# A linear-attention and two-layer feed-forward kernel: mish by tanh, arctan and sine in grouped table loads, 30 matmul tiles from float32 to fp32r, weights parked as two halves

## Chip, cores and metric

One Trainium2 chip, one of its cores. The time is device microseconds of one launch, from several runs of the same program; a profile is one further execution taken by the hardware profiler. Engines are called as the profile calls them: PE (matmul), PEld (its weight loads), DVE, ACT, POOL, SP (which issues the DMAs here).

## The reference

Inputs are float32 or wider: r, k, v of shape (4 batches, 8 heads, 768 steps, 48), decays w and bonuses u per head, and two feed-forward layers whose weights come in float64 (the kernel reads them as pairs of 32-bit words).

```python
# attention, per batch b and head h, state is 48x48
for t in range(768):
    cur = outer(u * k[t], v[t])
    y[t] = r[t] @ (state + cur)
    state = w[:, None] * state + outer(k[t], v[t])
x = y as (4 * 768 tokens, 384)
h = x @ w_in                       # 384 -> 2048
x = (h * tanh(log1p(exp(h)))) @ w_out     # mish, 2048 -> 384
h = maximum(x @ w2_in, 0)          # 384 -> 2048
out = (h * h) @ w2_out             # 2048 -> 384
```

## The kernel before

**Tiles and blocks.** The 768 steps are cut into six chunks c of 128; a chunk of all four batches is 512 tokens. The attention of a chunk is computed by units (chunk, batch), 24 in all. The feed-forward layers work on one chunk at a time: a *block* is (layer, chunk), and `BLOCKS` (L171) is their order: (1,0), (1,1), (2,0), (2,1), (1,2), (1,3), (2,2), ... and so on, so that two chunks pass through layer 1, then the same two through layer 2. A block has 16 *tiles* j of 128 hidden features (`NF` = 16). For tile i (numbered through all 192 of the kernel) `up` (L839) multiplies the tile's 128x384 weights by the 384x512 input into one PSUM buffer h; `act1` (L863) or `act2` (L905) does the activation on ACT and DVE; `down1` (L913) or `down2` (L949) multiplies its output by the tile's second weights and adds to three or four accumulators over the 16 tiles.

**Precision.** A float32 matmul of 512 columns shows as two records. The other way, `mm3` (L832), splits both operands into a high part, rounded to fp32r, and a low part (the rest): three fp32r matmuls, high by high, high by low, low by high. The split is `halves` (L892) for activations, ACT making the high copy (L896, L898) and DVE subtracting (L901); `split_w` (L375) for weights; `split_x` (L805) for a block's input. Two constants say what stays float32: `FULL_UP = (0,)` and `FULL_DOWN = (0, 1)` (L239). Block 0 is float32 in its ups (L848) and downs (L926); block 1 is fp32r in its ups and in the downs of tiles 0 to 7 and float32 in the downs of tiles 8 to 15. That is 16 up and 24 down tiles in float32, all others in fp32r.

**Mish.** Per 128x512 tile in `act1`:

```python
ACT e = exp(h / ws)                  # L880
ACT e = square(e + 1)                # L881, the 1 is a one-column tile
DVE e = min(e, SQ20) + 1             # L871
ACT r = ln(e)                        # L883
ACT r = exp(-r)                      # L884
DVE e = e * r                        # L885
DVE r = (e - 2) * r                  # L874
DVE g = (r + 0.5) * h                # L877, and half a factor later in finish1
```

Exp, ln, square and copy are all in one activation table, loaded once at the start (L279).

**Weights.** `convert` (L323) turns a tile's 768 weight columns from float64 words to float32: ACT scales the high word (L337) and extracts bits (L344, layer 1), DVE shifts and merges (L348 to L358). The raw tile comes by one DMA of 768 KB (L331). For layer 1 the float32 tile lands in the ring `wa` (pairs of tiles), where block 0 uses it directly; during block 0 it is also written to DRAM (`keep`, L383) and split for block 1. Raw tiles go through a ring `wb` of eight. Layer 2's weights are converted and split while block 1 and the first layer-2 block run (`make_w2`, L388), and both halves are parked in DRAM. When the order comes back to layer 1, `again_w1` (L396) loads the float32 tile and splits it again on ACT and DVE; `again_w2` (L404) loads the two halves in two DMAs.

**Attention.** A unit scales r and k (L439), forms scores on PE (L494), fills a diagonal tile (L469 on ACT, four records per fill; for chunk 0 every second on POOL), selects by mask (L505, DVE), multiplies (L543 to L605) and updates the state. `SPANS` (L173) says beside which feed-forward tiles a chunk's units are due: chunk 1 beside tiles 0 to 13. Chunk 0 comes first, with nothing beside it; its outputs x are copied from PSUM to a float32 tile (L644 on ACT, L646 on DVE).

**Order.** Every step is an item of a `Plan` (L80) with engine, estimated duration, due time and the tiles it reads and writes. `order` (L108) plays the engines through in time: when an engine is free it takes, of the items whose inputs are ready, the one with the smallest due time. The resulting list is the program order of each engine, SP's DMAs included. Tiles live in rings; an item that reuses a buffer waits for all users of the tile before it. Rings that matter here: `e` 3, `ghi` 3, `glo` 3, `wf` 2, PSUM `up` 2 and `flex` 1 for h, `at` 2 for attention. An up of tile i is due at i, its activation at i+1, its down at i+4 (`LAG`).

## Time and profile before

| what | value |
|---|---|
| three runs | 935.93, 936.21 (median), 936.94 us |
| profiled execution, span from first to last instruction | 935.9 us |
| first up matmul of block 0, of block 1, of block 2 | 34.61, 126.82, 199.68 us |
| last matmul starts | 928.88 us |
| busy: PE, PEld, DVE, ACT, POOL | 910.3, 734.7, 597.2, 619.4, 8.5 us |
| DMA | 114.00 MB, mean 122 GB/s |

A profile is read engine by engine and by stage. Busy time of PE is the union of matmul records whose ends are modelled, so the pace of a dense stretch is read from start to start. DVE and ACT records overlap a little with the next one. Stages here are cut at the first up matmuls of blocks 0, 1 and 2.

### The profile page before, as it was taken

To read this page: it belongs to the slowest core of one execution; us is meant where nothing else is said; L and a number is where in the kernel's file an instruction comes from. 1 tells how busy PE (TensorE), PEld (TensorE's weight loads), DVE (VectorE), ACT (ScalarE), POOL (GpSimd) and SP (SyncE) were. 2 spreads that over 40 slices of the span, in tenths; PEclk is the share of its full clock that TensorE was granted. 3 is DMA by queue.
4 is the path that set the end of the run, shared out by engine and by line. 5 is a ranking of instruction groups with operands and counts; after the bars stand their busy time and mean duration, and the time that the engine had idled before them with its cause. 6 is when DMAs were issued, how large, how long until landed. Compare 5 with 4: busy or idle time off the path is not lost.

```text
span 935.9 us, 13341 instructions
## 1 busy us (share of the span) xinstructions
PE 910.3 (97%) x5072; PEld 734.7 (78%) x5072; DVE 597.2 (64%) x981; ACT 619.4 (66%) x1126; POOL 8.5 (1%) x18
## 2 busy tenths in 40 slices
PE   3999999999999999999999999999999999999997
PEld 3645458768988888878888889888878888899996
DVE  6899999999544648688876332354777877211212
ACT  1897779777646767778777554667777877544442
POOL 2100000000000000000000000000000000000000
PEclk9999999999999999999999999999999999999999
DMA  9994153788423434010666220434100155200001
GB/s 247 348 333 139 44 173 132 244 268 311 171 79 113 139 113 130 1 54 1 216 212 213 80 71 1 131 100 130 51 9 1 68 202 178 92 1 1 34 1 39
DMA packets 40875, 114.00 MB, mean 122 GB/s; under 512 B 4609, under 2 KB 7938, under 8 KB 40802
## 3 DMA queue, kind: packets, MB, share of 16 engines
q1 hardware_dynamic: 40802, 113.06, 36.7%
q8 instruction: 42, 0.69, 0.3%
q14 instruction: 31, 0.25, 0.1%
HBM read 88.47 MB, written 23.59 MB: 120 GB/s over the span
## 4 chain that ended last, share of the span: by engine, by line
PE 92%; DVE 3%; ACT 1%; DMA 1%; issue 1%; SPq 0%; DVEq 0%
PE h L833 13%; PE h L835 13%; PE h L834 13%; PE acc L960 8%; PE acc L962 7%; PE acc L961 7%; PE acc L926 6%; PE acc L833 5%; PE acc L835 5%; PE acc L834 5%; PE h L848 3%; PE sc L494 2%; PE y L566 2%; DMA rk<-in_rk_dram 1%; PE y L543 1%
## 5 line engine op out<-in xcount | busy, mean ns | idle before, releaser
L901 DVE TENSOR_TENSOR glo<-g,ghi 128x512 fp32r<-128x512 f32 x96 | 66.3, 691 | 211.8 <-ACT ghi L896 211.5
L909 ACT ACTIVATE e<-h 128x512 f32<-128x512 f32 x96 | 57.3, 597 | 115.4 <-PE h L835 114.9
L896 ACT ACTIVATE ghi<-e 128x512 fp32r<-128x512 f32 x96 | 60.5, 630 | 57.0 <-PE acc L961 55.7
L833 PE MATMUL h<-xh_a,w 128*128 128x512 f32 x216 | 87.7, 406 | 2.1 <-DVE e L877 2.1
L880 ACT ACTIVATE e<-h 128x512 f32<-128x512 f32 x96 | 57.2, 597 | 47.8 <-PE h L835 42.3
L833 PE MATMUL acc<-ghi,w 128*128 128x512 f32 x216 | 86.1, 398 | 0.0
L835 PE MATMUL h<-xh_a,w 128*128 128x512 f32 x216 | 85.0, 394 | 0.0
L835 PE MATMUL acc<-ghi,w 128*128 128x512 f32 x216 | 84.7, 392 | 0.0
L834 PE MATMUL h<-xl_a,w 128*128 128x512 f32 x216 | 84.2, 390 | 0.0
L834 PE MATMUL acc<-glo,w 128*128 128x512 f32 x216 | 84.1, 389 | 0.0
L885 DVE TENSOR_TENSOR e<-e,r 128x512 f32<-128x512 f32 x96 | 65.9, 688 | 23.2 <-ACT r L884 22.8
L883 ACT ACTIVATE r<-e 128x512 f32<-128x512 f32 x96 | 60.2, 631 | 21.7 <-DVE e L871 21.6
L881 ACT ACTIVATE e<-e,one 128x512 f32<-128x512 f32 x96 | 69.5, 725 | 2.0
L469 ACT ACTIVATE A<-cst_sb,dg 128x128 f32<-128x128 f32 x176 | 55.9, 402 | 18.3 <-DVE dg L454 18.3
L874 DVE SCALAR_TENSOR_TENSOR r<-e,r 128x512 f32<-128x512 f32 x96 | 65.8, 687 | 1.6
L926 PE MATMUL acc<-g,wf 128*128 128x512 f32 x144 | 65.9, 595 | 0.0
L910 ACT ACTIVATE g<-e 128x512 f32<-128x512 f32 x96 | 60.7, 632 | 2.9
L901 DVE TENSOR_TENSOR glo<-e,ghi 128x512 fp32r<-128x512 f32 x72 | 49.4, 689 | 20.3 <-ACT ghi L898 18.7
L884 ACT ACTIVATE r<-r 128x512 f32<-128x512 f32 x96 | 60.2, 629 | 1.4
L898 ACT ACTIVATE ghi<-e 128x512 fp32r<-128x512 f32 x72 | 45.0, 626 | 12.5 <-DVE e L877 12.2
L833 PEld LDWEIGHTS h<-xh_a,w 128*128 128x128 f32 x216 | 40.5, 188 | 12.8 <-DVE e L877 3.6
L877 DVE SCALAR_TENSOR_TENSOR e<-r,h 128x512 f32<-128x512 f32 x72 | 49.1, 684 | 1.4
(291 smaller groups left out, 2102.4 us busy)
## 6 DMA issues: line engine op xcount, KB each, us to landing
raw<-in_w_dram SPq DMA_DIRECT2D x32, 768.0 KB, 5.9
nat<-in_nat_dram SPq DMA_DIRECT2D x24, 576.0 KB, 5.9
wk<-wd SPq DMA_DIRECT2D x32, 384.0 KB, 3.1
rk<-in_rk_dram SPq DMA_DIRECT2D x24, 448.0 KB, 5.5
wd<-wf SPq DMA_DIRECT2D x16, 384.0 KB, 7.4
wd2hi<-w SPq DMA_DIRECT2D x16, 384.0 KB, 5.0
wd2lo<-w SPq DMA_DIRECT2D x16, 384.0 KB, 3.8
out_dram<-o SPq DMA_DIRECT2D x24, 192.0 KB, 1.9
```

What stands on the lines that cost most here:

```text
L833: nc.tensor.matmul(o, wh, xh, start=first, stop=False, skip_group_check=True)
L834: nc.tensor.matmul(o, wh, xl, start=False, stop=False, skip_group_check=True)
L835: nc.tensor.matmul(o, wl, xh, start=False, stop=last, skip_group_check=True)
L874: nc.vector.scalar_tensor_tensor(r.ap, e.ap, 2.0, r.ap, ALU.subtract, ALU.mult)
L881: add("ACT", 0.73, d + 0.2, lambda: nc.scalar.activation(e.ap, e.ap, AF.Square, bias=one), r=[e, T_one], w=[e])
L885: add("DVE", 0.69, d + 1, lambda: nc.vector.tensor_tensor(e.ap, e.ap, r.ap, ALU.mult), r=[e, r], w=[e])
L901: lambda: nc.vector.tensor_tensor(lo.get(), g.ap, f32v(hi.ap), ALU.subtract), r=[g, hi], w=[lo],
L910: add("ACT", 0.63, d + 0.2, lambda: nc.scalar.activation(g.get(), e.ap, AF.Square), r=[e], w=[g])
L926: nc.tensor.matmul(o, ws_[0][:, sl], hi.ap, start=(j == 0), stop=(j == NF - 1), skip_group_check=True)
L960: nc.tensor.matmul(o, hi[:, sl], h_, start=(j == 0), stop=False, skip_group_check=True)
L961: nc.tensor.matmul(o, hi[:, sl], l_, start=False, stop=False, skip_group_check=True)
L962: nc.tensor.matmul(o, lo[:, sl], h_, start=False, stop=(j == NF - 1), skip_group_check=True)
```

## The change

In blocks 0 and 1 (tiles 0 to 31) mish is computed from t = (1 - tanh(x/2))/2, which is 1/(1 + e^x): tanh(log1p(e^x)) = (1 - t²)/(1 + t²) = cos(2 arctan t) = sin(pi/2 - 2 arctan t). Tanh, arctan and sine are not all in one table: three tables hold (tanh, arctan), (arctan, sine) and (sine, tanh). Tiles go in groups of 1, 1, six times 2 and six times 3; a group's tanhs, arctans and sines run as batches, and a pass over the finished program order puts a table load before a pass whose function the loaded table lacks, taking the table that lasts longest. Tanh then arctan then sine, repeated, takes three loads for two groups. Mish costs DVE one multiply per tile. From tile 32 on the mish is as before, with a bias of 1.0 given as an immediate.

Only the downs of tiles 0 to 9 stay float32 (`FULL`). For that block 0's input is split, and its weights. All layer-1 weights are split once, in `convert`, and both halves are parked in DRAM and loaded again as one tile of 768 KB; so are layer 2's. Each weight tile j has one buffer `w{j}` that holds first the raw words, then the two halves; the float32 form is in a ring `wf` of 6. Rings `e`, `ghi` and `glo` have 4. In block 1 h goes around five PSUM buffers (`up` 2, `flex` 1, `at` 2). The high copies of activations of tiles 0 to 31, of layer-1 weights 2 to 15, and every second diagonal fill of chunk 1 move from ACT to DVE. Options that were off are removed from the code.

```diff
+HALFPI = 1.5707963267948966
+GROUPS = (1, 1) + (2,) * 6 + (3,) * 6
+TRIG = sum(GROUPS)
+GROUP_OF = [(sum(GROUPS[:g]), n) for g, n in enumerate(GROUPS) for _ in range(n)]
+HIGH, WHIGH = 32, 2
+FULL = frozenset(range(0, 10))
...
+TABLES = (
+    ("sigmoid_and_others", "TA"), ("trig_and_small", "AS"), ("silu_and_others", "ST"),
+    ("natural_log_exp_and_others", "EL"),
+)
+def table_loads(items):
+    users = [it for it in items if it["table"]]
+    loads, k = {}, 0
+    while k < len(users):
...
+        best = max(TABLES, key=run)
+        loads[users[k]["n"]] = best[0]
+        k = run(best)
+    return loads
...
-        (w_p, "wa", NF // 2), (w_p, "wb", NF // 2),
-        (conv_p, "raw", 2), (conv_p, "wf", 2),
+        *((w_p, f"w{j}", 1) for j in range(NF)),
+        (conv_p, "wf", 6),
...
-        (f_p, "e", 3), (f_p, "r", 2), (f_p, "ghi", 3), (f_p, "glo", 3), (f_p, "o", 4),
+        (f_p, "e", 4), (f_p, "r", 2), (f_p, "ghi", 4), (f_p, "glo", 4), (f_p, "o", 4),
...
+        if layer == 1 and j >= WHIGH:
+            add("DVE", 0.56, due, lambda: nc.vector.tensor_copy(hi.get(), f.get()), r=[f], w=[hi])
+        else:
+            add("ACT", 0.87, due, lambda: nc.scalar.activation(hi.get(), f.get(), AF.Copy), r=[f], w=[hi])
         add(
-            "DVE", 0.15 + n, due + 0.5,
-            lambda: nc.vector.tensor_tensor(lo.get(), f.get()[:, cols], f32v(hi.get()), ALU.subtract), r=[f, hi], w=[lo],
+            "DVE", 0.96, due + 0.5,
+            lambda: nc.vector.tensor_tensor(lo.get(), f.get(), f32v(hi.get()), ALU.subtract), r=[f, hi], w=[lo],
         )
-    def keep(x, j, t, due):
-        d = kept[x, j] = fixed(wd[x][j], f"wd{x}_{j}")
-        it = add("SP", 0.393, due, lambda: dma(d.ap, t.get() if x == "1" else f32v(t.get())), r=[t], w=[d])
+    def keep(layer, j, due):
+        d = kept[layer, j] = fixed(wd[layer][j], f"wd{layer}_{j}")
+        t = W[layer, j][0].whole
+        it = add("SP", 0.786, due, lambda: dma(d.ap, f32v(t.get())), r=W[layer, j], w=[d])
...
+    def again(layer, j, due):
+        d = kept[layer, j]
+        t, hi, lo = parts(layer, j, "r")
+        add("SP", 0.786, due, lambda: dma(f32v(t.get()), d.ap), r=[d], w=[hi, lo])
...
+        if units[n][0] == 1 and not e:
+            def g():
...
+                nc.vector.tensor_tensor(
+                    A.get(), anti[:, None, :].to_broadcast([128, NP, C]), d[:, :, None].to_broadcast([128, NP, C]), ALU.mult
+                )
+            add("DVE", 0.69, due, g, r=[u["dg"], T_cst], w=[A])
+            return
...
+            def g():
+                a, o = (direct["all", x].get()[:, :, cols] for x in ("xh", "xl"))
+                i = y[0][:, 0:3 * C].rearrange("q (k t) -> q k t", t=C)
+                nc.vector.tensor_tensor(o, i, f32v(a), ALU.subtract)
+            add("DVE", 0.55, due, g, r=[y[0]] + direct["xh"], w=direct["xl"])
...
+    def turn(i, extra=0.0):
+        b = GROUP_OF[i][0] if i < TRIG else i
+        return b + 0.02 * (i - b) + extra
...
-        h = R["flex" if flex else "up"].new([128, 512], F32, f"h{i}")
+        name = ("up", "up", "flex", "at", "at")[i % 5] if NF <= i < TRIG else "flex" if flex else "up"
+        h = R[name].new([128, 512], F32, f"h{i}")
...
+        if i < TRIG:
+            add(
+                "ACT", 0.6, turn(i, 1),
+                lambda: nc.scalar.activation(e.get(), h.ap, AF.Tanh, scale=0.5 / ws), r=[h], w=[e], table="T",
+            )
...
+                def a():
+                    for _, x, _, _ in now:
+                        nc.scalar.activation(x.ap, x.ap, AF.Arctan, scale=-0.5, bias=0.5)
...
+                for k, (n, x, o, p) in enumerate(now):
+                    add(
+                        "ACT", 0.64 + (k == 0), -50 + i + 0.1 * k,
+                        lambda x=x: nc.scalar.activation(x.ap, x.ap, AF.Sin, scale=-2.0, bias=HALFPI), r=[x], w=[x],
+                        table="S",
+                    )
+                for n, x, o, p in now:
+                    add(
+                        "DVE", 0.69, turn(n, 2),
+                        lambda x=x, o=o, p=p: nc.vector.tensor_tensor(o.get(), x.ap, p.ap, ALU.mult), r=[x, p], w=[o],
+                    )
+                    late.append((n, o, None) if n in FULL else (n, *halves(n, o, turn(n, 2.2))))
...
+            if i < HIGH:
+                add("DVE", 0.42, due, lambda: nc.vector.tensor_copy(hi.get(), g.ap), r=[g], w=[hi])
...
-        add("PE", 2.6 if full else 2.08, i + LAG, f, r=list(w) + [x for x in (hi, lo) if x], w=a)
+        due = turn(i, GROUP_OF[i][1] + 0.5) if i < TRIG else i + LAG
+        add("PE", 2.6 if full else 2.08, due, f, r=list(w) + [x for x in (hi, lo) if x], w=a)
...
+    unit_ = 1 / ws ** 2 if i < TRIG else 2 / ws ** 2
...
+    ordered = plan.order(rings)
+    loads = table_loads(ordered)
+    for it in ordered:
+        if it["n"] in loads:
+            nc.scalar.preload_act_table_set(loads[it["n"]])
         it["fn"]()
```

## Rows read from the trace of the kernel before

**Rows 1.** The page's first part: engine, busy us, share of the span, instructions

```profile
PE 910.3 (97%) x5072; PEld 734.7 (78%) x5072; DVE 597.2 (64%) x981; ACT 619.4 (66%) x1126; POOL 8.5 (1%) x18
```

**Rows 2.** Waits of PE from 120 us: who waited for whom, total, times, longest

```profile
PE h L833 <- DVE e L877: 2.1, 3, 1.3
```

**Rows 3.** Stages: us, busy (instructions) of each engine, clock, DMA share, GB/s

```profile
0.00:34.60 34.60, 18.01 (x168) 15.24 (x168) 22.78 (x50) 13.46 (x29) 8.52 (x18) 1.00 0.95 297
34.60:126.90 92.30, 92.03 (x495) 45.76 (x495) 90.21 (x151) 79.83 (x151) 0.00 (x0) 1.00 0.59 196
126.90:199.70 72.80, 72.80 (x273) 50.73 (x271) 70.06 (x113) 57.56 (x94) 0.00 (x0) 1.00 0.58 199
199.70:929.00 729.30, 727.20 (x4142) 622.95 (x4140) 413.63 (x669) 468.35 (x854) 0.00 (x0) 1.00 0.30 96
```

**Rows 4.** Groups of PE, whole run: count, busy us, mean ns, idle before

```profile
L926 PE MATMUL acc<-g,wf 128*128 128x512 f32 x144 | 65.9, 595 | 0.0
L848 PE MATMUL h<-x,wf 128*128 128x512 f32 x96 | 44.6, 601 | 1.1 <-ACT x L644 0.9 <-DVE g L877 0.2
```

**Rows 5.** Timeline of PE: start us, us; two dense stretches

```profile
122.07 2.74 PE L848 MATMUL h<-x,wf 128*128 128x512 f32 x6
124.65 2.74 PE L926 MATMUL acc<-g,wf 128*128 128x512 f32 x6
...
147.32 0.40 PE L833 MATMUL h<-xh_a,w 128*128 128x512 f32 x1
...
151.47 0.40 PE L833 MATMUL h<-xh_a,w 128*128 128x512 f32 x1
```

**Rows 6.** Groups of DVE by shape, 34.6 to 126.9 us

```profile
L885 DVE TENSOR_TENSOR e<-e,r 128x512 f32<-128x512 f32 x15 | 10.3, 685 | 0.0
...
L380 DVE TENSOR_TENSOR w<-wf,w 128x768 fp32r<-128x768 f32 x8 | 7.5, 954 | 0.0
L871 DVE TENSOR_SCALAR e<-e 128x512 f32<-128x512 f32 x16 | 6.7, 420 | 1.2 <-ACT e L881 1.2
...
L380 DVE TENSOR_TENSOR wu<-wf,wu 128x384 fp32r<-128x384 f32 x7 | 3.8, 551 | 0.0
```

**Rows 7.** Timeline of DVE, back to back: start us, us

```profile
40.18 0.95 DVE L348 SCALAR_TENSOR_TENSOR wf<-wf,raw 128x768 uint32<-128x768 uint32 x1
41.05 0.42 DVE L871 TENSOR_SCALAR e<-e 128x512 f32<-128x512 f32 x1
41.39 0.96 DVE L355 SCALAR_TENSOR_TENSOR wf<-raw,wf 128x768 uint32<-128x768 uint32 x1
```

**Rows 8.** Groups of DVE, whole run: the one-input 768-column operation

```profile
L352 DVE TENSOR_SCALAR wf<-wf 128x768 uint32<-128x768 uint32 x16 | 8.9, 553 | 0.9 <-ACT wf L337 0.9
```

**Rows 9.** Groups of ACT, whole run

```profile
L910 ACT ACTIVATE g<-e 128x512 f32<-128x512 f32 x96 | 60.7, 632 | 2.9
...
L880 ACT ACTIVATE e<-h 128x512 f32<-128x512 f32 x96 | 57.2, 597 | 47.8 <-PE h L835 42.3 <-PE h L848 5.1
...
L279 ACT ACT_TABLE_LOAD x1 | 1.3, 1283 | 0.8 <-PEq L1315 0.8
```

**Rows 10.** Groups of ACT by shape, 34.6 to 126.9 us

```profile
L469 ACT ACTIVATE A<-cst_sb,dg 128x128 f32<-128x128 f32 x32 | 10.3, 448 | 1.6 <-DVE dg L454 1.6
...
L377 ACT ACTIVATE w<-wf 128x768 fp32r<-128x768 f32 x8 | 6.7, 844 | 0.0
L377 ACT ACTIVATE wu<-wf 128x384 fp32r<-128x384 f32 x8 | 3.8, 512 | 0.0
```

**Rows 11.** Timelines of DVE, ACT and PE at the first up projection

```profile
32.04 0.94 DVE L355 SCALAR_TENSOR_TENSOR wf<-raw,wf 128x768 uint32<-128x768 uint32 x1
...
34.20 0.36 ACT L644 ACTIVATE x<-y 128x256 f32<-128x256 f32 x1
...
34.61 2.84 PE L848 MATMUL h<-x,wf 128*128 128x512 f32 x6 [0.89 <-ACT x L644]
```

**Rows 12.** DMA issues: KB each, median us from issue to landing

```profile
raw<-in_w_dram SPq DMA_DIRECT2D x32, 768.0 KB, 5.9
```

More of the change, by code (lines that the diff above doesn't have):

```diff
@@ L87, in __init__, with add @@
         self.items, self.rate, self.latency = [], rate, latency
-    def add(self, eng, dur, due, fn, r=(), w=(), deps=(), late=0.0):
-        it = dict(n=len(self.items), eng=eng, dur=dur, due=due, fn=fn, deps=list(deps), after=[], ready=0.0, late=late)
+    def add(self, eng, dur, due, fn, r=(), w=(), deps=(), late=0.0, table=""):
+        it = dict(n=len(self.items), eng=eng, dur=dur, due=due, fn=fn, deps=list(deps), after=[], ready=0.0, late=late, table=table)
         for t in r:
@@ L531, in y_pe @@
         c, b = units[n]
[L532 removed]
+        ps = u["y"] = [R["at"].new([128, 512], F32, f"y{n}_{i}") for i in range(1 if not c else 2)]
         def out_y(p, y, m):
@@ L1069, in rwkv_moe_kernel @@
         for c2 in range(1, NCH):
             b1 = BLOCKS.index((1, c2))
-            if i == (SPANS[c2][1] + 1 if JOINT else NF * (b1 - 1)):
+            if i == NF * (b1 - 1):
                 spread(c2, NF * b1 - 4)
                 split_x(c2, NF * b1 - 3)
-    if WARM:
-        t = R["acc2"].tiles[0]
-        idle = Tl(None, (), None, "idle")
-        scratch = R["acc2"]
-        z = scratch.new([128, 512], F32, "warm")
-        scratch.tiles.insert(0, scratch.tiles.pop())
-        def warm():
-            nc.tensor.matmul(z.get()[:, 0:256], cst_sb[:, 0:128], cst_sb[:, 0:256], start=True, stop=True)
-        for k in range(WARM):
-            add("PE", 0.43, 1e6, warm, r=[T_cst], w=[z])["after"].append(U[3]["sums"])
```

356 lines of the change are left out of this document (124 added, 232 removed).

## The prediction

> **What bounds the kernel now.** I read the engines' busy times first: PE is busy for 910.3 of the 935.9 us span [rows 1]. A busy PE need not be the limit, so the waits of PE come next. After the first up projection PE idles 2.4 us in all [rows 3], and 2.1 of them are three waits of up projections for the mish multiply on DVE [rows 2]. So from the first up projection to the last matmul nearly every microsecond taken off PE comes off the time, if the others keep pace. Whether they do is read by stage [rows 3]. The stage from 34.6 us (first up matmul) to 126.9 us (first up matmul of block 1) is special: PE is busy for 92.03 of 92.30 us, DVE for 90.21, ACT for 79.83. There two engines stand at their limit at once. Later DVE loosens: 70.06 of 72.80 in the next stage, 413.63 of 729.30 in the rest.
>
> The profiled execution has a span of 935.9 us; the three timed runs lie between 935.93 and 936.94, so the median of 936.21 is 0.3 above that span, and I add 0.3 to sums made on the trace.
>
> **PE.** Before, 16 up tiles (96 records, six for a tile) and 24 down tiles (144 records) are float32 [rows 4]. After, only the downs of tiles 0 to 9 are: 40 less 10 is 30. In a dense stretch a float32 tile takes 2.58 us from start to start; an fp32r up and down together take 151.47 - 147.32 = 4.15 us, so 2.075 each [rows 5]. A moved tile gives back 0.505 us, 30 give **15.2 us**. Of these, 16 ups and the downs of tiles 10 and 11 lie in the stage up to block 1; the other 12 downs, 6.1 us, fall in block 1, where PE is the limit and DVE loses work (three mish operations of 0.60 a tile for one of 0.60, one of 0.34 and some residuals), so they count in full.
>
> **DVE up to block 1.** Records overlap: a 768-column operation recorded at 0.95 is followed after 0.87, a 512-column one of 0.42 after 0.34 [rows 7]. I therefore charge the recorded mean less 0.08, which makes 0.60 of the 0.685 of a 512-column operation on two tensors. Gone from this stage are the three operations of 0.60 of the mish, 15, 15 and 14 times (the first stands in [rows 6]) = 26.4, the 16 clamps at 0.34 = 5.4, and weight residuals that were made ahead for block 1: 8 x 0.87 and 7 x 0.47 = 10.3 [rows 6]. Sum -42.1. New: 16 residuals of whole weight tiles at 0.87 = 13.9, since now block 0 itself needs them; 14 high parts at 0.47 = 6.6, priced by the 768-column shift [rows 8]; one multiply at 0.60 for tiles 0 to 13 = 8.4; high and low parts of two tiles' outputs, 2 x (0.34 + 0.60) = 1.9; four diagonal fills taken from ACT at about 0.60 = 2.4; and of the four residuals of x, two at 0.47 = 0.9 (the first two fall in gaps before 30 us). Sum +34.1. DVE work comes to 90.2 - 42.1 + 34.1 = 82.2 us; with the 2.1 us that it idled before, it ends at 34.6 + 84.3 = 118.9. What no row shows is how much it idles when weights may run only six tiles ahead (the ring of six float32 tiles is held by the float32 downs) and results come in pairs. Nothing more is one end. The other is the ACT share: were DVE busy for only 79.83 of 92.30, as ACT was [rows 3], 82.2 us would take 95.0 and end at 129.6. I take 120, nearer to the row of DVE itself.
>
> **PE up to block 1.** It saves 16 x 0.505 = 8.1 on ups; it has done 12 downs in place of 13, ten of them float32, which is 10 x 2.58 + 2 x 2.075 = 30.0 against 33.5, 3.5 less. It starts later: the first up needs the first weight tile's two halves and x's two halves. Its float32 weight was ready near 33.0 (0.94 after 32.04) and the last piece of x near 34.56 (34.20 + 0.36), and the matmul began at 34.61 [rows 11]. Now a residual of x of 0.55 follows on a DVE that is also asked for a 0.95 residual of the weight and the next tile's bits: between 0.5 and 2.4 us later, I take 1.4. PE alone would then reach block 1 at 126.9 - 8.1 - 3.5 + 1.4 = 116.7. DVE's 120 is later, so DVE decides by **3.3 us**, and the PE saving of this stage shrinks by so much.
>
> **ACT up to block 1.** Mish falls from four passes to three; of its 62 passes in the stage some 45 stay. Tanh from PSUM I price by the exponential that does the same, 0.60, arctan and sine by a pass from buffer to buffer, 0.63 [rows 9]. No row shows tanh, arctan or sine; the bounds are 0.60 and, were each two such passes, 1.26. I take the lower, since exponential and square, unlike as they are, lie within 0.04. Eight groups (tiles 0 to 13) at three loads for two groups are 12 table loads at 1.28 [rows 9] = 15.4. Passes overlap by 0.11, so 17 fewer at 0.52 are -8.8; 16 weight copies go, eight at 0.73 [rows 10] and eight of half the width at about 0.40, -9.0; half the fills go, 16 x (0.45 - 0.11), -5.4 [rows 10]; two weight copies come, +1.5. Sum 79.8 - 23.2 + 16.9 = 73.5, below DVE's 82.2, so I cost it at nothing: DVE's longer list covers it by 8 us, and what ACT needs beyond that comes on top. The one row of a load is the first instruction of the engine and shows no emptying of the engine around it. By the Trainium skill, "ScalarE: Activation LUTs", section "What ACT_TABLE_LOAD costs", a switch takes about 2.66 us, 1.38 of them a drain; an estimate by that page would add 12 x 1.38 = 16.6, make ACT 90.1, more than DVE, and the sum about 932. By that page the row's 1.28 agrees with the load itself; no run here shows the drain yet.
>
> **Edits costed at nothing.** Reloaded layer-1 weights come as two parked halves, so 32 weight splits on ACT and DVE go: they lay beside PE in a stretch where DVE had room [rows 3], and PE did not wait for them [rows 2]. Their cover was PE's own matmuls; nothing returns. Their transfers double, as do the stores in block 0: there 18.1 MB moved at 196 GB/s, and 6.3 MB more make 264 GB/s against 297 in the stage before [rows 3]. A store waits on SP for its low half and holds up the loads of the next chunk queued behind it; no DMA is in the waits of PE now [rows 2]. If that cover were gone, a late input would cost one landing, 5.9 us [rows 12]. Deeper buffers, the Square without its bias tile and high parts on DVE lie beside PE as well. The three waits of 2.1 us come at fp32r up projections (line 833) whose chain is unchanged; with DVE relieved I take back 0.5, bounds 0 and 2.1.
>
> **Sum.** 936.2 - 15.2 + 1.4 (start) + 3.3 (DVE) - 0.5 = **925.2 us**. The bounds: every wait hidden gives 936.2 - 15.2 + 0.5 - 2.1 = 919.4; DVE at 129.6 gives 12.9 in place of 3.3, 934.8.
>
> **Rivals.**
> *PE stays the limit.* DVE keeps ahead, as in the stage before, where it was full and PE hardly waited [rows 2, 3]. Against it: the count above. Time 925.2 - 3.3 = 921.9, down to 919.4.
> *ACT becomes the limit through the tables.* If every load also empties the engine for as long again, a switch costs 12 x 1.28 = 15.4 more: ACT needs 88.9, with the idle share that DVE had 91.0, and reaches block 1 at 125.6 instead of DVE's 120: 930.8. The page above states such a drain. For it: loads stand between dependent passes. Against it: the only load in the trace shows nothing of the kind.
> *The change does not do all it says.* If passes of different groups mix so that each kind loads anew, or loads are put in besides the planned ones, three per group in place of one and a half, there are 42 loads for 21, 12 of the extra ones before block 1: the same 930.8, told apart by the count of loads.
> *Slower: the group chain stops PE.* In block 0 three h buffers serve groups of two, so the second up projection of a pair needs the buffer that the first multiply of the pair before releases. From the end of a pair's last up: tanh 0.6, load 1.3, two arctans 1.15, sine 0.63, multiply 0.68 [rows 6, 9], some 0.7 of handing over, 5.1 us. PE has one up and two downs to do meanwhile, 2.08 + 2 x 2.58 = 7.2 us. But each hop can find its engine inside an operation of 0.95 or behind several. The chain decides from 7.2 us; if queueing doubles it to 10.2, it costs 3.0 in each of seven groups, 21 us in place of DVE's 3.3: 942.9. Groups of three in block 1 have five buffers and 10.4 us of cover. Against it: the group's operations carry early due times, and attention's matmuls stand between some pairs.
>
> **Chances.** The forecast, with DVE and hand-over costs between 922 and 929: 0.55. PE-bound at 919 to 922: 0.16. ACT or extra loads, 929 to 934: 0.11. The chain: 0.18, of which 0.13 end above 938 and 0.05 near 936. Two tenths of a per cent, 1.9 us, is about what this measurement can tell from no change. So faster 0.82, within 0.05, slower 0.13. The range takes in all but the chain's slow part and a little below the floor: 919 to 937.
>
> **What would show it.** Right: 60 float32 down records and no float32 up; the first up of block 1 near 120 us with DVE full and PE idle for some 5 us between its first up and there; 21 to 23 table loads of 1.28; no PE waits after 127 beyond 2 us. Wrong: ACT as the releaser of long PE waits before block 1 (tables), or idle of 1 us or more ahead of the up projections in each pair, ended by the multiply (chain), or a stop of PE on a DMA.

## The result, and the profile after

The changed kernel takes **927.67 us** (median of four runs, 926.27 to 928.72) beside 936.46 us (935.93 to 936.94) before: a ratio of **0.9902 [0.9888, 0.9916]**, 8.8 us. Two later measurements of the same kernel gave 0.9889 and 0.9888 (below), so the change is worth some 9 to 11 us. The forecast was 925.2, a ratio of 0.988. The profiled execution has a span of 926.0 us and took 927.75; every run of this study lies 1.7 to 1.9 us above its span. That of before, at 935.9, therefore stands for some 937.7, about 1 us above the median beside it.

The first part of the page after (engine, busy us, share, instructions), which answers to [rows 1]:

```profile
PE 896.6 (97%) x5162; PEld 752.9 (81%) x5162; DVE 548.7 (59%) x911; ACT 578.6 (62%) x1047; POOL 8.8 (1%) x17
```

PE, DVE and ACT each have less to do, by 13.7, 48.5 and 40.8 us. The stages of after, cut at the first up matmuls of blocks 0, 1 and 2 (us, then busy time of PE, PEld, DVE, ACT, POOL, then the granted clock, DMA share, GB/s), answer to [rows 3], though the cuts stand elsewhere:

```profile
0.00:37.13 37.13, 18.01 (x168) 15.99 (x168) 25.49 (x53) 12.95 (x28) 8.78 (x17) 0.95 0.96 324
37.13:123.38 86.25, 82.63 (x543) 55.34 (x543) 83.52 (x132) 73.18 (x115) 0.00 (x0) 0.98 0.63 226
123.38:191.65 68.27, 68.27 (x298) 55.76 (x297) 48.07 (x80) 53.78 (x80) 0.00 (x0) 1.00 0.62 219
191.65:926.00 734.35, 727.65 (x4156) 625.78 (x4154) 391.57 (x650) 438.70 (x826) 0.00 (x0) 1.00 0.35 118
```

From first up to first up, before and after, with two more executions of the changed kernel (after_again and after_third):

| stage, us | before | after | after_again | after_third |
|---|---|---|---|---|
| to the first up of block 0 | 34.61 | 37.13 | 34.88 | 36.91 |
| to the first up of block 1 | 92.21 | 86.25 | 86.30 | 84.77 |
| to the first up of block 2 | 72.86 | 68.27 | 68.28 | 68.28 |
| to the end of the span | 736.2 | 734.35 | 734.0 | 734.0 |

Block 1 gives 4.6 us in every execution, the first stage 6 to 7.4, the rest 2; the start takes back between 0.3 and 2.5. The waits of PE of after, from 22 us to the end (who waited for whom, total, times, longest), which answer to [rows 2]:

```profile
PE h L774 <- DVE w L394: 2.1, 2, 1.2
PE sc L500 <- DVE A L509: 2.0, 1, 2.0
PE h L772 <- ACT w L391: 1.7, 1, 1.7
PE h L772 <- DVE g L834: 1.5, 1, 1.5
PE h L772 <- DVE e L847: 0.2, 1, 0.2
```

All but the last 0.2 us lie before 62 us: the scores of the last unit of chunk 0 (`sc`), the first up (for the high part of the first weight tile, then for its low part), and one up at 61.29 us that needs the h of a pair whose multiply (L834) is late. From 62 us to the first up of block 1 PE is busy without a gap. There is no DMA among the releasers.

The new work on ACT, from the first up to the first up of block 1 (count, busy us, mean ns, idle before), beside [rows 9, 10]:

```profile
L1043 ACT ACT_TABLE_LOAD x13 | 16.7, 1283 | 0.2
...
L809 ACT ACTIVATE e<-h 128x512 f32<-128x512 f32 x15 | 8.9, 595 | 7.7 <-PE h L774 7.6
L819 ACT ACTIVATE e<-e 128x512 f32<-128x512 f32 x14 | 8.2, 628 | 0.0
L828 ACT ACTIVATE e<-e 128x512 f32<-128x512 f32 x14 | 8.1, 620 | 0.0
```

Tanh takes 595 ns, arctan 628, sine 620: what exponential and square took. Of the 13 loads twelve belong to tiles 0 to 13; the whole run has 23, besides the one at its start. What a load costs around itself is read from ACT's timeline (start us, us):

```profile
40.10 1.72 ACT L350 ACTIVATE wf<-raw 128x768 f32<-128x768 f32 x2
41.84 1.28 ACT L1043 ACT_TABLE_LOAD   x1
43.13 0.60 ACT L809 ACTIVATE e<-h 128x512 f32<-128x512 f32 x1
```

The load begins 0.02 us after the pass before it ends (40.10 + 1.72 = 41.82), and the next pass 0.01 us after the load ends. The group of these 23 loads, with 0.4 us of idle before all of them:

```profile
L1043 ACT ACT_TABLE_LOAD x23 | 29.5, 1283 | 0.4
```

DVE in the same stage, beside [rows 6, 8]:

```profile
L394 DVE TENSOR_TENSOR w<-wf,w 128x768 fp32r<-128x768 f32 x16 | 15.2, 951 | 0.0
...
L389 DVE CAST w<-wf 128x768 fp32r<-128x768 f32 x14 | 7.7, 553 | 0.1
L834 DVE TENSOR_TENSOR g<-e,h 128x512 f32<-128x512 f32 x10 | 6.7, 682 | 0.2 <-ACT e L828 0.2
```

These are the 16 residuals, the 14 high parts and the multiplies that the sum had charged, at the durations it had charged.

### The profile page after: what moved, and what is told of

The parts are those of the page before. It is cut to its first block, busy times and chain, and to the rows that moved or that the text cites. A ratio compares the mean times of both kernels' runs of the same rounds, so it can differ in the third digit from the quotient of the medians.

```text
span 926.0 us, 13282 instructions
## 1 busy us (share of the span) xinstructions
PE 896.6 (97%) x5162; PEld 752.9 (81%) x5162; DVE 548.7 (59%) x911; ACT 578.6 (62%) x1047; POOL 8.8 (1%) x17
## 4 chain that ended last, share of the span: by engine, by line
PE 91%; DMA 6%; DVE 1%; SPq 0%; ACT 0%; issue 0%
PE h L772 14%; PE h L774 14%; PE h L773 14%; PE acc L933 8%; PE acc L935 7%; PE acc L934 7%; PE acc L772 6%; PE acc L774 6%; PE acc L773 6%; DMA raw<-in_w_dram 3%; DMA rk<-in_rk_dram 2%; PE acc L896 2%; PE y L570 2%; PE sc L500 2%; PE y L547 1%; PE y L603 1%
## 5 line engine op out<-in xcount | busy, mean ns | idle before, releaser
L854 DVE TENSOR_TENSOR e<-e,r 128x512 f32<-128x512 f32 x64 | 44.0, 689 | 23.4 <-ACT r L853 23.0
L868 ACT ACTIVATE ghi<-e 128x512 fp32r<-128x512 f32 x64 | 40.1, 628 | 15.6 <-DVE e L847 15.2
L844 DVE SCALAR_TENSOR_TENSOR r<-e,r 128x512 f32<-128x512 f32 x64 | 44.1, 690 | 1.5
L933 PE MATMUL acc<-w,ghi 128*128 128x384 f32 x128 | 44.2, 345 | 0.0
L772 PE MATMUL h<-xh_a,w 128*128 128x512 f32 x96 | 41.0, 427 | 3.2 <-ACT w L391 1.7
L935 PE MATMUL acc<-w,glo 128*128 128x384 f32 x128 | 43.2, 337 | 0.0
L934 PE MATMUL acc<-w,ghi 128*128 128x384 f32 x128 | 43.1, 337 | 0.0
L500 PEld LDWEIGHTS sc<-rk 48*128 48x128 f32 x384 | 25.7, 198 | 21.4 <-DVE A L509 8.1
L500 PE MATMUL sc<-rk 48*128 48x128 f32 x384 | 30.8, 298 | 12.0 <-DVE A L509 7.2
L509 DVE COPY_PREDICATED A<-cst_sb,sc 128x512 f32<-128x512 int32 x48 | 33.3, 730 | 14.1 <-PE sc L500 14.0
L850 ACT ACTIVATE e<-e 128x512 f32<-128x512 f32 x64 | 40.2, 630 | 1.5
L774 PE MATMUL h<-xh_a,w 128*128 128x512 f32 x96 | 38.7, 403 | 2.1 <-DVE w L394 2.1
L435 DVE TENSOR_TENSOR rk<-rk,E 112x1024 f32<-112x1024 f32 x24 | 30.1, 1259 | 17.9 <-DMA rk<-in_rk_dram 17.9
```

What stands on the lines that cost most here:

```text
L500: nc.tensor.matmul(ps[e][:, p, :], u["rk"][q, 1, p, :], u["rk"][q, 0, p, :], start=True, stop=True)
L772: nc.tensor.matmul(o, wh, xh, start=first, stop=False, skip_group_check=True)
L774: nc.tensor.matmul(o, wl, xh, start=False, stop=last, skip_group_check=True)
L933: nc.tensor.matmul(o, hi[:, sl], h_, start=(j == 0), stop=False, skip_group_check=True)
L934: nc.tensor.matmul(o, hi[:, sl], l_, start=False, stop=False, skip_group_check=True)
L935: nc.tensor.matmul(o, lo[:, sl], h_, start=False, stop=(j == NF - 1), skip_group_check=True)
```

## Experiments

### The start: a residual that holds up DVE's queue

First the changed kernel again, beside the variants on the same chip.

> The changed kernel once more, on the chip of the three runs beside it: 927 to 928.5 us. Both theories expect the first up projection near 37 us, the first of block 1 near 123.4, and a lower granted clock in two short stretches (30 to 35 us and 61 to 65 us), as in its first profile.

Measured: 925.67 us (925.19 to 926.90) beside 936.64, ratio 0.9889 [0.9871, 0.9906]. The first up came at 34.88 us and that of block 1 at 121.18, 2.2 us earlier than expected; the two stretches of lower clock are there, each as much earlier.

What made the start late is on DVE's timeline of after (start us, us, idle before and its releaser):

```profile
22.73 1.32 DVE L509 COPY_PREDICATED A<-cst_sb,sc 128x512 f32<-128x512 int32 x2
25.09 0.56 DVE L652 TENSOR_TENSOR xl_a<-y,xh_a 128x384 fp32r<-128x384 f32 x1 [1.05 <-ACT xh_a L643]
25.57 0.54 DVE L450 TENSOR_REDUCE dg<-nat 128x8 f32<-128x384 f32 x1
...
28.39 1.33 DVE L509 COPY_PREDICATED A<-cst_sb,sc 128x512 f32<-128x512 int32 x2
```

The first residual of x (L652) stands in DVE's order ahead of the reduction `dg` of the next unit. It waits 1.05 us for ACT's high part, and the reduction, which waits for nothing, stands behind it; then come the fills that need `dg`, the selects, the scores. The edit changes the order alone:

```diff
+    behind(U[0]["xl"], U[3]["dgit"])
     loads = table_loads(ordered)
```

`behind` takes the first item out of the ordered list and puts it behind the second: the residual of batch 0's x goes behind the reduction of unit 3.

> One instruction of DVE is moved: the first residual of x (batch 0) is issued behind the reduction of unit 3 in place of before that of unit 2. No work is added or taken. Theory A (a wait in order): DVE stood 1.05 us for ACT's copy with units 2 and 3 queued behind it, so chunk 0 ended 1.9 us later than before, and PE ran part of it at the lower clock. Then the last y of chunk 0 ends near 33.5 us, the first up starts at 35 to 36, and the time falls by 1.5 to 3 us against the changed kernel. Theory B (the volume of DVE's work up to block 1 decides): the time stays within 0.7 us, since the volume is the same.

Measured: 924.40 us (922.10 to 925.53), ratio 0.9875 [0.9858, 0.9891]: 1.3 us faster, a little less than theory A had. The first up came at 33.37 us. DVE of late_xl, same view:

```profile
25.01 0.55 DVE L450 TENSOR_REDUCE dg<-nat 128x8 f32<-128x384 f32 x1
25.48 0.55 DVE L652 TENSOR_TENSOR xl_a<-y,xh_a 128x384 fp32r<-128x384 f32 x1
25.94 1.32 DVE L509 COPY_PREDICATED A<-cst_sb,sc 128x512 f32<-128x512 int32 x2
```

No idle is left ahead of the residual. Between this run and the first of the changed kernel the intervals overlap, so it was run again on another chip:

> The kernel of late_xl once more: the changed kernel with one residual of x moved behind the reduction of unit 3 in DVE's program order. Theory A (the residual's wait in DVE's order cost the start 1 to 3 us in the changed kernel): the ratio to the kernel before lies below the three of the changed kernel (0.9902, 0.9889, 0.9888), at 0.985 to 0.988, the wait of the scores for the filled diagonal is 1.0 us or less, and the granted clock from 40 to 65 us is 0.97 or more. Theory B (the first run of this edit only met earlier landings of the first loads; the start scatters by 3 us between executions of one kernel anyway): the ratio lies at 0.988 to 0.991, among those of the changed kernel.

Measured: 923.55 us (922.44 to 924.69), ratio 0.9861 [0.9844, 0.9878]; the wait of the scores is 0.8 us, the granted clock from 40 to 65 us is 1.00. Theory A holds in all three numbers. The two ratios of this edit lie below all three of the changed kernel, by some 0.25% or 2.3 us.

The steps of the start, read from the timelines, say why. Columns: from the scores of chunk 0's third unit to those of its fourth; from these to the first up; the granted clock in that last stretch; and from the very first score to the first up.

| kernel | third to fourth | to first up | clock | first score to first up |
|---|---|---|---|---|
| before | 3.38 | 6.91 | 1.00 | 22.12 |
| after | 4.71 | 7.96 | 0.78 | 25.05 |
| after_again | 4.71 | 7.92 | 0.79 | 24.32 |
| after_third | 4.71 | 6.65 | 1.00 | 24.66 |
| late_xl | 3.41 | 6.66 | 1.00 | 22.21 |
| late_xl_again | 3.47 | 6.67 | 1.00 | 22.21 |
| start_order | 3.22 | 6.59 | 1.00 | 23.36 |

The third step is 4.70 to 4.72 us in all nine profiles of kernels without the edit and 3.22 to 3.47 in all four with it: the queue's stop costs **1.3 us**. The wait of the scores is followed by a lower clock in six of those nine profiles, those in which it lasted 2.0 us; in the other three it lasted 1.1 to 1.7. In the stretch after it the same matmuls take 6.12 us of PE in after and 4.50 in late_xl. The stretch from the fourth scores to the first up in after (columns as in the table of stages; the clock is the third number from the end):

```profile
29.17:37.10 7.93, 6.12 (x64) 5.55 (x64) 5.92 (x10) 5.48 (x11) 0.64 (x2) 0.78 1.03 402
```

The same stretch in late_xl:

```profile
26.71:33.40 6.69, 4.50 (x65) 3.94 (x65) 6.02 (x10) 5.86 (x12) 0.18 (x1) 1.00 1.03 400
```

After PE's idle from 27.1 to 29.17 us in after its matmuls ran for a while at the lower of the two levels. Where that happens the start costs 1.3 us more. The first two steps, ahead of the edit, scatter as well: from the first to the third scores before took 11.8 us, after 12.4, after_again 11.7, after_third 13.3, the two of late_xl 12.1.

Two attempts to shorten what is left. In late_xl_hi0 the first weight tile's high part goes to DVE too; in start_order the split of that tile is placed by hand in DVE's order as well:

```diff
-            add("ACT", 0.87, due, lambda: nc.scalar.activation(hi.get(), f.get(), AF.Copy), r=[f], w=[hi])
+            add("ACT", 0.87, due, lambda: (nc.vector.tensor_copy(hi.get(), f.get()) if (layer, j) == (1, 0) else nc.scalar.activation(hi.get(), f.get(), AF.Copy)), r=[f], w=[hi])
...
+    behind(first_w["hi"], first_w["s3"])
+    behind(first_w["lo"], U[3]["xl"])
```

The first edit is in both (the plan still counts the item as ACT's; DVE runs it at that place of the list). The two moves are in start_order alone: there the high part goes right behind the last merge of the same tile's words, the low part behind the last residual of x, which leaves one operation on the second tile ahead of it.

> As late_xl, and the high part of the first weight tile is made by DVE (0.47) in place of ACT (0.83 behind three other passes). Theory A: the first up starts another 0.5 to 1.5 us earlier and the time falls by up to as much. Theory B: DVE has 0.47 more to do, the time stays or rises by 0.5.

> As late_xl_hi0, and DVE makes the high and the low part of the first weight tile before it merges the second tile's words. Only DVE's order changes. If PE at the start waits for these two results in their place in the queue, the first up starts 0.5 to 1.5 us earlier relative to the end of chunk 0 and its wait for the low part (1.2 us) goes, but the second up still waits for the same DVE work: the time falls by 0 to 1 us against late_xl_hi0, to 921 to 923. If DVE's volume at the start decides alone, nothing changes.

Measured: late_xl_hi0 922.28 us (922.19 to 924.98), ratio 0.9857 [0.9836, 0.9879], which can't be told from late_xl's 0.9875 and 0.9861; its first up comes 7.00 us after the fourth scores, not sooner. Start_order 926.22 (923.84 to 928.11), ratio 0.9889 [0.9874, 0.9904], no better than the changed kernel. Its last step, 6.59 us, is not shorter either. In PE's timeline of start_order the wait ahead of the first up has changed its releaser:

```profile
35.90 0.50 PE L774 MATMUL h<-xh_a,w 128*128 128x512 f32 x1 [1.85 <-ACT xh_a L644]
```

With the weight ready the last piece of x is what the first up waits for, and the edit itself moved that piece back. DVE of start_order:

```profile
34.67 0.56 DVE L392 CAST w<-wf 128x768 fp32r<-128x768 f32 x1
35.14 0.28 DVE L646 CAST xh_a<-y 128x128 fp32r<-128x128 f32 x1
```

DVE's share of x (L646) now stands behind the high part and begins 5.83 us after the fourth scores, in late_xl 5.17. The step from first to second scores took 8.13 us in this execution against 6.87 in late_xl. That step scatters between 6.5 and 8.1 us over the executions of all the variants (5.9 in the one profile of before) and lies ahead of the edit. In start_order DVE waits longer for a landing there:

```profile
17.09 1.22 DVE L436 TENSOR_TENSOR rk<-rk,E 112x1024 f32<-112x1024 f32 x1 [1.48 <-DMA rk<-in_rk_dram]
```

The same operation in late_xl comes 2.3 us sooner:

```profile
14.78 1.30 DVE L435 TENSOR_TENSOR rk<-rk,E 112x1024 f32<-112x1024 f32 x1 [0.68 <-DMA rk<-in_rk_dram]
```

So this execution lost most of the 2.5 us of its start (first up at 35.90 us against 33.37) to landings. That is less than half of the 6.0 us between the two profiles. Another 2.9 lie behind the first up: the stage to block 1 takes 87.58 us against 84.71, with a wait of 2.2 us for a multiply of DVE that ends at 61.35 us and a granted clock of 0.53 from there to 65 us. Such a stretch of lower clock is in after too, without the edit; whether the edit has a part in the worse ratio is open. The best kernels of the study are thus late_xl and late_xl_hi0, at 922.3 to 924.4 us.

> The changed kernel beside start_order on one chip: 925 to 928.5 us, from the first up to block 1 86.3 us, from there to block 2 68.3 us; the start of the first up may differ by some microseconds with the landing of the first loads.

Measured: 925.64 us (924.26 to 927.12), ratio 0.9888 [0.9873, 0.9903], the same as after_again. The stage to block 1 took 84.77 us, 1.5 less than expected. The profiles of late_xl say what these 1.5 us are. The same stage in late_xl_again, at the full clock throughout:

```profile
33.70:118.38 84.68, 80.95 (x542) 54.16 (x543) 83.27 (x132) 73.18 (x115) 0.00 (x0) 1.00 0.69 248
```

In late_xl the clock was low for the first 6.7 us of that stage, and yet it took 84.71 us:

```profile
33.40:40.10 6.70, 6.00 (x26) 4.05 (x27) 6.70 (x11) 6.67 (x9) 0.00 (x0) 0.50 1.03 400
```

DVE is busy for all of these 6.7 us. What PE lost there came back: its wait for the multiply, which ends near 57.6 us, is 0.9 us in late_xl and 1.7 in late_xl_again. So the lower clock ahead of a wait for DVE cost nothing, in late_xl as in after_third. Behind the last such wait, near 61 us in after, it cost in full: the stage took 86.25 and 86.30 us in after and after_again.

### How many float32 downs: which engine binds in block 0

```diff
-FULL = frozenset(range(0, 10))
+FULL = frozenset()
```

```diff
-FULL = frozenset(range(0, 10))
+FULL = frozenset(range(0, 16))
```

Full_none has the first line, full_16 (all downs of block 0 in float32) the second.

> No tile is float32 any more: the downs of tiles 0 to 9 are fp32r too. PE gets 10 x 0.505 = 5.05 us less, DVE 10 x (0.34 + 0.60) = 9.4 us more, all before block 1. Theory B (DVE is the limit up to block 1, at 79.4 of 82.1 us): the first up of block 1 moves from 123.4 to 129 to 131, the time rises by 4 to 8 us. Theory C (after the start PE is the limit, DVE is full but in time): block 1 begins at 118 to 120 and the time falls by 3 to 5 us.

> Downs of tiles 10 to 15 are float32 as well. PE gets 6 x 0.505 = 3.0 us more (two of the six before block 1), DVE 6 x 0.94 = 5.6 us less (1.9 before block 1). Theory B (DVE still decides up to block 1): that stage shortens by 1 to 2 us, block 1 lengthens by 2.0, the time stays within 1.5 us of the changed kernel (925.7 to 927.7). Theory C (at ten tiles PE is already the limit from 65 us on): the time rises by 2.5 to 3.5 us, to 929 or 930.

Measured: full_none 933.61 us (931.88 to 935.10), ratio 0.9968 [0.9956, 0.9981]; full_16 928.45 (927.15 to 929.81), ratio 0.9913 [0.9897, 0.9930]. Full_none takes 10 x 0.505 = 5 us off PE, and the stage to block 1 grows from 86.25 to 93.84 us: each output that is no longer float32 wants a high part (0.34) and a residual (0.60) from DVE, 9.4 us for ten. From 65 to 119 us PE then stands still for 6 of 54 us, at a granted clock of 0.91, and DVE for 0.6. That stretch in full_none:

```profile
65.00:119.00 54.00, 47.87 (x342) 36.98 (x340) 53.42 (x91) 37.56 (x64) 0.00 (x0) 0.91 0.39 143
```

The same stretch in full_16:

```profile
65.00:119.00 54.00, 54.00 (x375) 34.84 (x374) 50.29 (x83) 45.78 (x78) 0.00 (x0) 1.00 0.44 154
```

The waits of PE in full_none name DVE nearly throughout:

```profile
PE y L547 <- DVE A L509: 3.5, 4, 2.1
PE acc L773 <- DVE glo L871: 1.8, 3, 0.8
```

Full_16 goes the other way: 87.29 us to block 1 and 70.27 to block 2, 1.0 and 2.0 more than after_again. That is two and four tiles at 0.505, so every float32 tile counts in full and DVE's relief brings nothing: PE binds there, from 62 us on, as theory C had it. At ten float32 tiles the two limits lie close together. As an estimate, full_none's stage less DVE's 9.4 gives 84.4 us; PE's own list of some 80.6 (92.2 - 8.1 - 3.5; 80.95 busy in late_xl_again) with the 3.6 us of its early waits gives 84.2. The numbers of float32 tiles between none, ten and sixteen were not run.

### The table loads: twice as many, and groups of one

```diff
+            nc.scalar.preload_act_table_set("natural_log_exp_and_others" if it["n"] != min(loads) else "sqrt_and_others")
             nc.scalar.preload_act_table_set(loads[it["n"]])
```

That is loads_twice, one more load ahead of each planned one (its trace has 23 and 22). Groups_of_one:

```diff
-GROUPS = (1, 1) + (2,) * 6 + (3,) * 6
+GROUPS = (1,) * 32
```

> Every planned table load is preceded by a load of another table, 22 more in all, 12 of them before block 1: 15.4 us more of ACT there, which then has about 85 us of work in the 82 us of the stage. Theory A (loads of 1.28 lie beside other work as long as ACT's volume fits): the time rises by 1 to 5 us. Rival (each load lies in the chain from the last up of a group to its first multiply, and PE waits for it): 14 groups get 1.28 to 2.57 us later each, the time rises by 15 us or more, and PE waits for the multiply in each group.

> Blocks 0 and 1 in groups of one tile: 18 table loads more than the changed kernel, about half of them before block 1 (11 to 12 us of ACT), but each group's chain from tanh to multiply has the same one or two loads and fewer passes. If doubling the loads cost 16 us because each chain grew longer, this costs 0 to 3 us. If it cost them because ACT's volume no longer fits before block 1, the stage up to block 1 grows by 4 to 8 us here too, and block 1, where ACT has room, stays at 68.3 us.

Measured: loads_twice 942.72 us (939.43 to 943.11), ratio 1.0052 [1.0032, 1.0073], slower than before the change; groups_of_one 931.45 (929.87 to 933.27), ratio 0.9956 [0.9940, 0.9971]. My theory A for loads_twice, that 22 more loads cost 1 to 5 us since ACT has room, fell: they cost 15 to 17 (15.3 by the ratios 1.0052 and 0.9889, 17 by 942.72 less 925.6), some 0.7 us for each 1.28. The stage to block 1 takes 7.5 us more than after, and block 1 6.4 more:

```profile
37.34:131.09 93.75, 86.97 (x543) 57.90 (x544) 83.02 (x130) 86.88 (x126) 0.00 (x0) 0.93 0.59 210
131.09:205.76 74.67, 70.34 (x298) 56.59 (x296) 48.57 (x81) 65.17 (x90) 0.00 (x0) 0.98 0.57 201
```

PE has as many matmuls as in after (543 and 298). It idles 7.5 us more in the two stages together, and it is busy 6.4 us more, at a granted clock of 0.93 and 0.98 in place of 0.98 and 1.00. So of the 15.1 us between the two profiles nearly half are slower matmuls. Where ACT has no room is seen from 40 to 65 us in loads_twice (ACT's busy time is the fourth), against 22.50 of the same 25 us in after_third:

```profile
40.00:65.00 25.00, 21.75 (x135) 14.41 (x134) 19.61 (x27) 24.84 (x32) 0.00 (x0) 0.90 1.03 367
```

There ACT is full and DVE is not. Elsewhere ACT has some room (48.76 of 54 us busy from 65 to 119 us), and there PE's waits (loads_twice, from 34 us) end with multiplies that a group's chain makes late:

```profile
PE h L772 <- DVE e L834: 4.3, 2, 2.3
PE h L772 <- DVE g L834: 2.9, 1, 2.9
PE h L772 <- ACT w L391: 1.5, 1, 1.5
PE sc L500 <- ACT e L819: 1.3, 1, 1.3
```

These sum to 10 us, 1.5 of them ahead of the first up as in after, over five places and not one per group. Groups_of_one puts the same kind of load in at another place: 40 loads in place of 23, but a chain of one tile only. Its group of loads:

```profile
L1043 ACT ACT_TABLE_LOAD x40 | 51.3, 1283 | 0.7
```

The 17 additional loads cost 5.8 us (931.45 less 925.64), 0.34 us each. By stage:

```profile
36.44:123.71 87.27, 83.66 (x552) 55.96 (x552) 83.87 (x133) 83.61 (x125) 0.00 (x0) 1.00 0.63 227
123.71:197.26 73.55, 71.11 (x315) 56.68 (x313) 57.36 (x89) 65.44 (x88) 0.00 (x0) 1.00 0.70 255
```

Neither of the two cases that I had set up came as stated. The stage to block 1 is 2.5 us longer than in after_third, and one fp32r down more (2.08) lies in it, so eight additional loads, 10.3 us of ACT, cost next to nothing there, although ACT is as full from 40 to 65 us (24.79 of 25) as in loads_twice. Block 1, where ACT is not full, is 5.3 us longer, with 2.4 us of idle PE and one unit's scores more in it; after it the run is 2.8 us shorter. (The edit also moves the due times of a tile's steps, so the cuts do not part quite the same work.) A full ACT between 40 and 65 us is therefore not by itself what a load costs. What the runs show is waits at a few places and, in loads_twice, the lower clock behind them: without the slower matmuls loads_twice pays 8.7 us, 0.40 a load, near the 0.34 here. That the waits come from the longer chain of a group, from tanh to multiply, fits their releasers and was not tested by itself. Sharing the loads in groups, against groups of one, is worth those 5.8 us.

### The old mish under the new precision

In this kernel blocks 0 and 1 use the exponential and logarithm form again, all else as changed.

```diff
-GROUPS = (1, 1) + (2,) * 6 + (3,) * 6
+GROUPS = ()
...
-        return [(i, *halves(i, e, d + 1.4))]
+        return [(i, g, None) if full else (i, *halves(i, e, d + 1.4))]
```

> The changed kernel, with blocks 0 and 1 computing mish as before (exp, square, ln, exp and four operations on DVE), singly and without table loads; float32 tiles, weights and rings as changed. DVE gets 14 x 1.8 + 16 x 0.34 - 14 x 0.6 = 22 us more before block 1. If the new mish is what makes room on DVE for the split weights, the first up of block 1 comes 18 to 25 us later and the time is 942 to 952. If DVE has that much room anyway, the time is within 3 us of 926.

Measured: 958.93 us (958.34 to 960.16), ratio 1.0239 [1.0222, 1.0257]. It is 33 us slower than the changed kernel and 22 slower than before; the stage to block 1 takes 109.03 us, as expected, and block 1 79.42, so block 1 lost more than I had counted. A stretch of block 1 in old_mish:

```profile
119.00:190.00 71.00, 65.38 (x309) 50.32 (x310) 69.06 (x123) 46.16 (x78) 0.00 (x0) 1.00 0.43 151
```

The waits of PE in the same profile, from 34 us:

```profile
PE acc L896 <- DVE g L847: 9.6, 6, 2.2
PE h L772 <- DVE e L847: 6.5, 6, 1.9
```

DVE is full and its multiplies are the releasers. So the other edits, the 30 tiles in fp32r among them, are worth nothing without the new mish. Part of DVE's load are the high copies that the change moved from ACT and that this kernel leaves on DVE: 14 of weights at 0.47 and 22 of activations at 0.34 make some 14 us, an estimate from the sum's prices. Taken off in full they would not bring 22 us back; that was not run. Nor was the other half, the new mish with all 40 tiles in float32: that it gains nothing alone is argued from PE, busy for 92.03 of 92.30 us before, and not shown.

### The removed splits, put back as ghosts

Each reload of a layer-1 weight is followed by a copy on ACT and a subtraction on DVE whose result nobody uses.

```diff
+        if layer == 1:
+            f = R["wf"].new([128, 768], F32, f"gh{j}")
+            add("ACT", 0.87, due + 2, lambda: nc.scalar.activation(f.get(), f32v(hi.get()), AF.Copy), r=[hi], w=[f])
+            add(
+                "DVE", 0.96, due + 2.5,
+                lambda: nc.vector.tensor_tensor(f.get(), f.get(), f32v(lo.get()), ALU.subtract), r=[f, lo], w=[f],
+            )
```

> After each of the 32 reloads of a layer-1 weight tile, ACT copies and DVE subtracts 128x768 elements into a spare buffer, as the old split did; nothing waits for the result. If the 2.1 us of waits of up projections for the mish multiply on DVE after 300 us went because these splits went, they come back: 1 to 2.5 us of such waits and as much time. If they went through the deeper rings or the reload as such, PE's waits after 200 us stay under 0.5 us and the time is that of the changed kernel within 0.7.

Measured: 927.10 us (925.78 to 929.51), ratio 0.9892 [0.9875, 0.9908], which can't be told from the changed kernel's 0.9889. In its profile the last stage takes 735.28 us against 734.0 to 734.35, and one wait after 200 us, at 374 us, is longer than in after (0.2), for the same multiply as in [rows 2] (line 877 of before):

```profile
PE h L779 <- DVE e L854: 0.6, 1, 0.6
```

That is 1 us at most, as a sign and not as a measurement: the edits costed at nothing lay beside PE. The traces also say where the late gain lies. Cut at the first ups of all blocks, one block holds it: 649.19 to 722.88 us in before, 73.69 us, with waits of 0.49 and 1.31 us in it:

```profile
692.11 0.50 PE L833 MATMUL h<-xh_a,w 128*128 128x512 f32 x1 [0.49 <-DVE e L877]
697.82 0.53 PE L833 MATMUL h<-xh_a,w 128*128 128x512 f32 x1 [1.31 <-DVE e L877]
```

In after it takes 71.3 us, without a wait, and in ghost_splits 71.3 as well, though the ghosts' work runs on ACT and DVE before it and into it. So the work of the removed splits is not what made PE wait there. Deeper rings, the Square with an immediate bias (630 ns in place of 725) and the reload as one tile remain, untested.

## Why the prediction was right, and which of its steps were not

The forecast of 925.2 lies 2.5 us below the first median and within 0.5 us of the two later ones; the range held, and its likeliest case, a gain limited a little by DVE, was the one that came. Step by step:

**PE, 15.2 us: right.** No float32 up is left, 60 float32 down records remain, and each moved tile counts 0.505. Block 1 shows it best: nine of the twelve float32 downs lie between its cuts in before (three at 129 to 139 us, six from 176 on), 9 x 0.505 = 4.5, and the stage gave 4.6. Full_16 took back 1.0 and 2.0 us for two and four tiles.

**DVE's and ACT's lists: right.** DVE was forecast at 82.2 us for the stage and has 83.52 busy; ACT at 73.5 and has 73.18. The prices of tanh, arctan and sine, taken at the lower bound, were 0.60 and 0.63; they measured 0.595, 0.628 and 0.620.

**DVE decides by 3.3 us: right in size, wrong in place.** The sum had DVE run to 120 us and PE wait for it at the end. PE's waits between its first up and block 1 make 3.6 us (2.1 for low parts of weights, 1.5 for a multiply), all released by DVE, but they lie before 62 us, while the first weights are made and the first pairs pass; after that PE never waits and is itself the limit. The step that failed is to read a whole stage's busy time as one limit. DVE had 52 of 54 us to do from 65 to 119 us and was in time; early on it was late. At the full clock (late_xl_again) PE idles 3.7 us in the stage, so the size holds there too. The first up of block 1 came at 123.38, 121.18 and 121.68 us in place of 120, since the stage began later and lost another 1.7 us in after, about as much in after_again: behind the wait that ended at 61.29 us nine matmuls stand 0.43 us apart in place of 0.23 (3.74 us in place of some 2.1), and the granted clock from 61.29 to 65 us is 0.54. No step of the sum held a price for that.

**Start, 1.4 us: too small, and its reason was wrong.** From first score to first up the change costs 2.2 to 2.9 us (24.32 to 25.05 against 22.12). The sum charged the weight's and the last piece's residuals; it costed "the first two" residuals of x at nothing, since they "fall in gaps before 30 us". That step failed: an instruction that falls in a gap also closes it to what stands behind it, when it waits itself. The first residual waits 1.05 us and stops the next unit by 1.3; in after and after_again the fallen clock behind it adds 1.3 more. In after_third it does not; there 1.5 of the 2.5 us lie ahead of the residual, in the first two steps. With the residual elsewhere the start costs 0.1 us against the one profile of before, so the terms that the sum did charge cost about nothing together.

**Late waits, 0.5 of 2.1: too small.** All but 0.2 us went, and the last stage shrank by 1.9 to 2.2 us although it has one fp32r down more and two float32 downs less (29, 30 and 31 against 30 and 31, about 1.05 us more on PE). Some 1 us beyond the waits is unexplained: the block of the two waits gave 2.4 us where they made 1.8, block 2 lost 0.7 where the downs made 1.05, and the end behind the last matmul's start gave 0.2. The work of the removed splits did not cause the waits (ghost_splits); which edit ended them stays open.

**Sum.** Against the forecast of -11.0 the profile of after gives -9.9: start 1.1 worse, the waits by DVE 0.3 worse, the clock 1.7 worse, the late stage some 2 better (waits of 1.9 taken back in place of 0.5, and some more that is unexplained). The 0.3 us that the sum put on top of the span compares a median with another, slower execution; differences between spans, as here, are free of it. The errors offset each other in part: that the forecast lies within 0.5 us of two medians is in part luck.

**The rivals.** *PE stays the limit* is half true, from 62 us on. *Tables*: ACT's timeline shows loads of 1283 ns and 0.02 us of idle ahead of one. The Trainium skill, "ScalarE: Activation LUTs", section "What ACT_TABLE_LOAD costs", adds a drain of 1.38 us to a switch; this trace shows none, 23 times (0.4 us of idle before all 23), and the measurement decides. By the Trainium skill's price the sum would have been about 932, an estimate. But loads_twice is this rival played out: if loads did cost double, the kernel would have taken 942.7 us and been slower than before, not 930.8 as I had worked out. I had 5.6 us more before block 1 and nothing behind it; the run shows 7.5 and 6.4. I let ACT's excess show only against DVE's list, left out the loads of block 1, and had no price for the clock behind the new waits. *More loads than planned*: there are 23. *The group chain stops PE*: it did so once in block 0, for 1.5 us: the multiply of a pair began at 60.55 us, 1.0 us after its sine had ended, behind three operations on weights (L367, L394, L389) that DVE took first. So 1.0 of the 1.5 us is queueing, as the rival had it, in one place of seven.

## What to carry to other kernels

Where two engines stand at their limit, a change that relieves one of them by loading the other gains nothing by itself: old_mish, which takes the work off PE and puts it on a DVE that keeps its old mish, is 22 us slower than before, and full_none, which takes still more off PE, gives 6 to 8 us of the gain back. The point where both run out together (near ten float32 tiles here, none and sixteen being slower) is found by trying both sides of it. An operation costed at nothing because it falls in a gap must be asked what stands behind it on its engine: if it waits, the gap is no longer free, and moving it by a few places gave the 1.3 us back here. To compare starts between executions, count from the first instruction that depends on the first load, not from zero. And a slower PE is not always a longer run: what it loses ahead of a wait for another engine comes back in that wait.

## What the runs showed of the hardware that was not expected

The granted clock fell behind short waits of PE: after idle of 2.0 us (27.1 to 29.17) it was 0.66 from 30 to 35 us, after 1.5 us (to 61.29) 0.54 from 61.29 to 65 us, the matmuls in between at the lower level of 1.2 GHz. It did not fall behind every such wait: in late_xl_again waits of 2.1 and 1.7 us ahead of the first up and of the multiply's up, and in groups_of_one waits of 1.7 and 2.1 us, left it at 1.00. The falls in after cost 1.3 and 1.7 us, about as much as the waits before them; that behind the first up in late_xl (0.50 from 33.4 to 40.1 us) cost the stage nothing.

The first loads land at times that differ by 2.2 us between executions: the first DVE operation on rk, right behind one that waits for the landing of nat, began between 9.03 and 11.27 us, in before at 11.22. The next step, from the first to the second scores, scattered by another 1.6 us over the variants. A first up at 34.53 us in one profile and at 37.91 in another is therefore no verdict on the kernels.

A table load of 1283 ns follows the pass before it and precedes the next within 0.02 us, two loads in a row as well; arctan and sine (628 and 620 ns) run at about the pace of an exponential (597).
